# Layer 1's first feed-forward group: tiles 6 and 7 through seven block products instead of two plain projections

## The chip, the core and the metric

The kernel runs on one core of a Trainium2 chip, eight of which share the chip. A core has TensorE (matmuls into PSUM, eight banks of 512 fp32 columns), VectorE, ScalarE, GpSimd and SyncE, which work side by side, each through its own instructions in order, and DMA engines that move data between the chip's memory (HBM) and the on-chip SBUF. Nearly all transfers are issued from SyncE's queue (SP), which also runs in order. The metric is the device time of one execution in microseconds (us), the median over the runs.

## The reference

Two kinds of layers alternate, twice each, on x of 2048 tokens by 640 features in fp32: a linear attention with 32 heads of 20, and a feed-forward layer of width 1728 with squared ReLU. Both use the same weights each time.

```python
def attention(x, wqkv, wo):
    q, k, v = heads(x @ wqkv)                       # 32 heads of 20
    phi = lambda t: where(t > 0, t + 1, exp(t)) + 1e-6
    pq, pk = phi(q), phi(k)
    kv = einsum("bhsd,bhse->bhde", pk, v)
    z = einsum("bhsd->bhd", pk)
    den = einsum("bhqd,bhd->bhq", pq, z)[..., None] + 1e-6
    o = einsum("bhqd,bhde->bhqe", pq, kv) / den
    return merge(o) @ wo

def feed_forward(x, w1, b1, w2, b2):
    h = x @ w1 + b1
    return maximum(h, 0) ** 2 @ w2 + b2

for _ in range(2):
    x = x + attention(layernorm(x), wqkv, wo)
    x = x + feed_forward(layernorm(x), w1, b1, w2, b2)
```

## The kernel before

**Precision.** Matmuls take fp32 operands as pairs of a high part (rounded by a copy on ScalarE) and a low part (the difference, on VectorE); a product is three matmuls: high by high, high by low, low by high. "High half" and "low half" below mean these two copies.

**Tiles and groups.** A tile is 128 tokens; 16 tiles form 4 groups (g = 0 to 3) of 4. In a layer the attention first goes through all tiles for phi(k) and phi(q), storing phi(q) in HBM (`pqd`). A transition then makes kv and folds it with wo into one 640 x 640 matrix M, of which five row blocks `M[0..4]` are kept as high and low halves. The output projection of a tile is phi(q), divided by its denominator and transposed, times M. Group 0's four tiles are projected in the transition. The later groups are projected inside the feed-forward stage of the group before, between its chunks.

**A group's feed-forward.** The first stage runs 14 chunks (c = 0 to 13, `fc1` at L1336) of 128 hidden units, 15 matmuls of 512 columns each (10 in the last), each followed by two activations on ScalarE (`act`, L1357). The second stage runs 28 steps (`fc2_step`, L1581), seven products by four units, on sums of hidden blocks. Their weights come through a ring of six buffers of 640 KB (`load_ring`, L387), in the order that `uses_of` (L224) lists; a load is issued on SP as soon as a buffer's last matmul is done. In group 0 of each layer, seven further units are loaded once and stay (`load_stay`, L415).

**The order of the other work** is written by hand: `at(g, n, f)` (L1639) hangs a piece of work behind chunk n of group g (or behind step n - 14 of the second stage), and `("pe", n)` hangs matmuls directly behind chunk n, ahead of the rest. Pieces on one place run in the order of their registration, which is: the bias additions, the mixing of M (`mix_M`), the feed-forward's own splits, the single tiles, the pairs. "Step n" below is the place behind chunk n. `after(g)` (L1700) turns negative steps into steps of the stage before, except in group 0, where they become step 0.

**A tile of the next group** goes through: `b_load_pq` (phi(q) from HBM into one of eight buffers shared with other tiles of the same size, tag "f", L121), `b_den` (two instructions on VectorE), `b_blocks` (the division and a transpose of 32 x 32 blocks on VectorE), `blocks_move` (L520; 16 copies of 32 x 160 on ScalarE, in quarters of four), the split into halves, the projection, the addition to x, the layer norm, and a trip through HBM that spreads it for the next group's first stage.

- *Single* (`single`, L1660): tile i of a group is projected by 30 matmuls of 320 columns, behind chunk `b = OUTS[i]` = 4, 7, 10 or 13. Its phi(q) is loaded at b - 8, the denominator comes at b - 6, blocks and the first two quarters at b - 5, the others at b - 4, the halves at b - 3 and b - 2.
- *Pair* (`pair`, L1730, and `pairs`, L1845): tiles 2j and 2j + 1 of the group are taken as the upper and lower row of a 2 x 2 block matrix, two 128-column blocks wide to a block, M's first 512 rows as another 2 x 2; seven products of sums (a Strassen-Winograd form) replace eight, and the last 128 columns of phi(q) by `M[4]` ("rest") are added in plain form: 6 + 6 + 3, 6 + 9, 6 + 9, and 9 matmuls of 320 columns, behind chunks c0 + 4 to c0 + 7, where c0 = `PAIR_AT[j]` = 1 or 6. Sums of token blocks are made on VectorE and split in the steps from c0 + 1 on; sums of M's blocks come from HBM: units m6, m7 and m4 through the ring, and m5 in the place of M's right half columns (`place`).

**Mixing.** `mix_M(g)` (L1865) makes those sums of M once in a layer, on VectorE and GpSimd with scratch in hidden and x buffers, splits them and stores them to HBM, in steps 1 to 6 of group `MIX_G[layer]` when that is 0. `place` then loads m5 over M's right half.

**Which tiles are pairs** is set by `PAIR_FROM[layer]` = (group, j), L62: from there on, pairs. In layer 0 it is (1, 1), with the mixing in the same group 1: in that group two singles, then one pair. In layer 1 it was (1, 0), with the mixing in group 0: all four tiles of group 0's stage (tiles 4 to 7 of the layer) are singles, and `place` waits for the second stage.

Of the kernel before, what the change touches and what calls it, by code (L numbers as in the profile page):

```python
# [21 lines left out]
TG = 4  # L22
# [34 lines left out]
PQ_AT, DEN_AT, TURN_AT = (-7, -5, -3, -1), (-3.5, -1, 1, 3), (-2.5, 0, 2, 4)  # L57
# [1 line left out]
    ((-2, 0), (-1.5, 1), (-1, 2), (-0.5, 3)), ((0, 0), (1, 1), (1, 2), (2, 3)),  # L59
    ((3, 0), (4, 1), (5, 2), (5, 3)), ((6, 0), (6, 1), (7, 2), (7, 3)),  # L60
)
MIX_G, PAIR_FROM = (1, 0), ((1, 1), (1, 0))  # L62
BLOCKS = 5


def unit_range(k):
    return 2 * k, min(2 * k + 2, KH)
# [7 lines left out]
def kernel(  # L75
# [25 lines left out]
    def bank(i, n=1):  # L101
        return PS[:, 512 * i : 512 * (i + n)]
# [17 lines left out]
    def ftile(name):  # L120
        return tmp.tile([P, D], F32, tag="f", name=name, bufs=F_BUFS)  # L121
# [136 lines left out]
    for m in ORDER:  # L258
        for k in range(PAIRS):
            a, b = unit_range(k)  # L260
# [183 lines left out]
    def ln_stats(t, xt):  # L444
        st = small.tile([P, 2, 6], F32, tag="bn", name="bn")
        for j in range(2):
            nc.vector.bn_stats(st[:, j], xt[:, j * HD : (j + 1) * HD])
        mv = small.tile([P, 2], F32, tag="mv", name="mv")
        nc.vector.bn_aggr(mv, st)  # L449
        rs = small.tile([P, 1], F32, tag="rs", name="rs")  # L450
        (nc.vector if t == ("a", 0) and not xT else nc.gpsimd).tensor_scalar(  # L451
            rs, mv[:, 1:2], LN_EPS, None, op0=ALU.add
        )
        nc.gpsimd.tensor_tensor(out=rs, in0=rs, in1=neghalf, op=ALU.pow)
        sts[t] = mv, rs
# [64 lines left out]
    def blocks_move(yz, js):  # L520
        if len(yz) == 1:
            yz.append(ftile("z"))
        yv, zv = (a.rearrange("p (c j q) -> p c j q", c=DC, q=B32) for a in yz)
        for j in js:
            for i in range(P // B32):
                nc.scalar.activation(  # L526
                    zv[j * B32 : (j + 1) * B32, :, i, :], yv[i * B32 : (i + 1) * B32, :, j, :], AF.Copy
                )
# [29 lines left out]
    def mm3(ps, lh, ll, rh, rl, first, last):  # L558

        seq = [(lh, rh), (ll, rh), (lh, rl)]  # L560
        for i, (a, b) in enumerate(seq):
            nc.tensor.matmul(ps, a, b, start=first and i == 0, stop=last and i == 2)  # L562
# [58 lines left out]
    for layer in range(N_LAYERS):  # L621
# [157 lines left out]
        pq, xr, pT, yzp, yzx, xn = {}, {}, {}, {}, {}, {}  # L779
# [3 lines left out]
        def b_load_pq(t):  # L783
            if t < NT:
                pq[t] = ftile("pqt")
                nc.sync.dma_start(pq[t], pqd[t])
# [9 lines left out]
        def b_load_x(t):  # L796
            xr[t] = x1_at(t)
            nc.sync.dma_start(xr[t], src[t])
# [24 lines left out]
        def b_step(t, n=1):  # L823
            for _ in range(n):
                next(b_gen.setdefault(t, b_ops(t)), None)

        def b_den(t):
            b_step(t, 2)

        def b_blocks(t):  # L830
            b_step(t, 3)
# [121 lines left out]
        for t in range(NT):  # L953
# [54 lines left out]
            g = list(range(DC)) if t > 0 else []  # L1008
# [154 lines left out]
        def run_side(n=1):  # L1163
            for _ in range(min(n, len(side_work))):
                side_work.pop(0)()
# [129 lines left out]
        wu.free = 1 if layer == 0 else 3  # L1295
        wu.load_ring()
        b_load_pq(4)
        run_side(2)
        for i in (2, 3):
            po[i] = bank((2, 4)[i - 2], 2)  # L1300
# [29 lines left out]
        def f_bias(t):  # L1330
            nc.gpsimd.tensor_tensor(out=xr[t], in0=xr[t], in1=b2bc, op=ALU.add)
# [287 lines left out]
        def p_split(t, first=0):  # L1619

            u = pTs[:, t % 2]
            v = yzp[t][1]
            nc.scalar.activation(u[:, 0], v, AF.Copy)
            yield
            nc.vector.tensor_tensor(out=u[:, 1], in0=v, in1=u[:, 0].bitcast(F32), op=ALU.subtract)
            pT[t] = u
# [12 lines left out]
        def at(g, n, f):  # L1639
            events.setdefault((g, n), []).append(f)  # L1640
# [19 lines left out]
        def single(g, i):  # L1660

            t, b = TG * (g + 1) + i, OUTS[i]

            on = after(g)
            if t > TG:
                on(b - 8, lambda: b_load_pq(t))
            on(b - 6, lambda: b_den(t))
            on(b - 5, lambda: b_blocks(t))
            on(b - 5, lambda: blocks_move(yzp[t], (0, 1)))
            on(b - 4, lambda: blocks_move(yzp[t], (2, 3)))  # L1670
            sp = p_split(t)
            on(b - 3, lambda: next(sp, None))
            on(b - 2, lambda: next(sp, None))
            on(b - 3, lambda: b_load_x(t))
            ps = []

            def out():
                yzp.pop(t)
                for j in range(2):
                    s = slice(j * HD, (j + 1) * HD)  # L1680
                    ps.append(bank(6 + j)[:, :HD])
                    for c in range(DC):
                        a = pT[t][:, :, c * P : (c + 1) * P]
                        mm3(ps[j], a[:, 0], a[:, 1], M[c][:, 0, s], M[c][:, 1, s], c == 0, c == DC - 1)
                pT.pop(t)

            def add():
                for j in range(2):
                    v = xr[t][:, j * HD : (j + 1) * HD]
                    nc.vector.tensor_tensor(out=v, in0=ps[j], in1=v, op=ALU.add)  # L1690
                ln_stats(("b", t), xr[t])

            at(g, ("pe", b), out)
            on(b + 1 + 0.5 * (i == 3), add)
            on(b + 2, lambda: norm_out(t))
            on(b + 3, lambda: f_bias(t))

            x_in(g, i)

        def after(g):  # L1700
            def on(n, f):
                if n < 0 and g > 0:
                    at(g - 1, NF + N_STEPS + 2 * n, f)
                elif n >= NF:
                    at(g, NF + int(2 * (n - NF)), f)
                else:
                    at(g, max(n, 0), f)

            return on

        def norm_out(t):
            xn[t] = ftile("xn")
            ln_apply(("b", t), xn[t], xr[t])
            xd[t] = spread_out(xn.pop(t))

        def x_in(g, i):
            t = TG * (g + 1) + i

            def load():
                yzx[t] = spread_in(xd.pop(t))  # L1720

            n = NF + (1, 5, 9, 13)[i]
            at(g, NF + (0, 3, 7, 11)[i], load)
            steps(lambda: x_split(t), (g, n + 4), (g, n + 5), (g, n + 6))
# [120 lines left out]
        def pairs(g):  # L1845
            on = after(g)
            js = [j for j in range(2) if (g, j) >= PAIR_FROM[layer]]
            both = [pair(g, j) for j in js]
            for p in both:
                next(p)  # L1850
            for i, moves in enumerate(MOVES_AT):
                if i // 2 not in js:
                    continue
                t = TG * (g + 1) + i
                on(PQ_AT[i], lambda t=t: b_load_pq(t))
                on(DEN_AT[i], lambda t=t: b_den(t))
                on(TURN_AT[i], lambda t=t: b_blocks(t))
                for n, q in moves:
                    on(n, lambda t=t, q=q: blocks_move(yzp[t], (q,)))
                on(PAIR_AT[i // 2] + 1, lambda t=t: b_load_x(t))  # L1860
                x_in(g, i)
            for p in both:
                next(p, None)
# [136 lines left out]
        for g in range(NG - 1):  # L2000
            for i in [i for i in range(TG) if (g, i // 2) < PAIR_FROM[layer]]:
                single(g, i)
            if (g, 1) >= PAIR_FROM[layer]:
                pairs(g)
# [69 lines left out]
```

## Time and profile before

| | |
|---|---|
| median of 3 runs | 1308.28 us (1307.75 to 1308.47) |
| profiled execution's own time | 1307.57 us |
| its span | 1305.9 us |
| TensorE busy | 1300.7 us (100%) |
| VectorE / ScalarE / GpSimd busy | 964.2 / 748.0 / 239.1 us |
| layer 1, group 0, first stage | 898.79 to 962.94 us of the span |
| layer 1, group 0, second stage | 962.94 to 1005.18 us |

In the profile's lines PE is TensorE, PEld its weight loads, DVE VectorE, ACT ScalarE, POOL GpSimd and SPq the queue of SyncE. A line of the timeline has start and length in us, engine, line of the kernel, operation, output and input by the program's names, shapes, and in brackets how long the engine was idle before and what ended that. L526 is `blocks_move`, L517 the block transpose, L562 a single's matmuls, L1806 a pair's, L1351 a chunk's, L1595 the second stage's. The chain of work that ended last is followed back from the end of the execution through what released each piece.

### The profile page before, as it was taken

The page shows a single profiled execution, that of the slowest core. Times are in us where ns is not written, and L with a number is a line of the kernel's source. Part 1 is how long each engine was busy: PE and PEld are TensorE (multiplying, and loading weights), DVE is VectorE, ACT ScalarE, POOL GpSimd, SP SyncE. Part 2 cuts the span into 40 slices and gives each one's busy share as a digit, 9 for nine tenths or more (in the row PEclk, how much of TensorE's full clock was granted, in tenths as well). Part 3 has the DMA queues.
Part 4 walks back from the last instruction along what each step waited for, and adds up shares of the span by engine and source line. Part 5 has one row for each costly group of instructions (what it writes and reads, how often), then busy time and mean ns, then how long its engine had stood idle before and what let it go on. Part 6 is the DMA issues. An engine that isn't in the chain of part 4 may idle for free.

```text
span 1305.9 us, 21566 instructions
## 1 busy us (share of the span) xinstructions
PE 1300.7 (100%) x7534; PEld 1189.1 (91%) x7534; DVE 964.2 (74%) x1788; ACT 748.0 (57%) x1663; POOL 239.1 (18%) x304
## 2 busy tenths in 40 slices
PE   9999999999999999999999999999999999999998
PEld 8888899989988988998988889999899899889998
DVE  8888978767975976933867877587779479579565
ACT  5988958785385486334323332397755934944342
POOL 2333310064031102101012222102330030021000
PEclk9999999999999999999999999999999999999999
DMA  6898985699997986998968666544889779779976
GB/s 196 251 279 266 309 264 171 256 352 383 329 330 252 324 333 234 300 371 286 346 212 235 210 173 175 149 174 174 318 293 367 275 252 330 297 249 318 355 269 220
DMA packets 155426, 355.06 MB, mean 272 GB/s; under 512 B 18406, under 2 KB 77670, under 8 KB 154678
## 3 DMA queue, kind: packets, MB, share of 16 engines
q1 hardware_dynamic: 148086, 331.39, 74.7%
q0 software_dynamic: 7232, 22.29, 6.6%
q8 instruction: 60, 0.98, 0.3%
q14 instruction: 48, 0.39, 0.1%
HBM read 265.76 MB, written 76.02 MB: 262 GB/s over the span
## 4 chain that ended last, share of the span: by engine, by line
PE 100%; POOL 0%; DVE 0%; issue 0%; ACT 0%; POOLq 0%
PE PS L1351 26%; PE PS L1595 26%; PE PS L654 21%; PE PS L562 12%; PE PS L1806 4%; PE PS L589 3%; PE PS L1467 3%; PE PS L703 2%; PE PS L1197 1%; PE PS L1185 1%; PE PS L976 1%; PE PS L715 0%; PE PS L463 0%; PE PS L1138 0%; PE PS L478 0%; DVE x L1609 0%
## 5 line engine op out<-in xcount | busy, mean ns | idle before, releaser
L1351 PE MATMUL PS<-xTb,u 128*128 128x512 f32 x1490 | 345.8, 390 | 0.0
L1351 PEld LDWEIGHTS PS<-xTb,u 128*128 128x128 f32 x1490 | 277.8, 188 | 56.1 <-issue 0.3
L654 PE MATMUL PS<-kq,xT 128*128 128x320 f32 (+2 forms) x1575 | 283.9, 334 | 0.0
L654 PEld LDWEIGHTS PS<-kq,xT 128*128 128x128 f32 x1575 | 250.3, 188 | 27.5 <-DVE rl L675 1.0
L1595 PE MATMUL PS<-u,arena 128*128 128x320 f32 x1644 | 250.6, 309 | 0.0
L1595 PEld LDWEIGHTS PS<-u,arena 128*128 128x128 f32 x1644 | 243.4, 188 | 0.4
L526 ACT ACTIVATE z<-y 32x160 f32<-32x160 f32 x512 | 171.1, 334 | 41.5 <-DVE y L517 35.5
L1567 ACT ACTIVATE arena<-R 128x512 fp32r<-128x512 f32 (+1 forms) x200 | 115.4, 591 | 122.4 <-PE PS L1595 84.7
L1576 DVE TENSOR_TENSOR arena<-R,arena 128x512 fp32r<-128x512 f32 (+1 forms) x200 | 136.2, 688 | 45.3 <-ACT arena L1567 43.3
L562 PE MATMUL PS<-kh,xh 128*128 128x512 f32 x480 | 124.3, 393 | 0.0
L451 POOL TENSOR_SCALAR rs<-mv 128x1 f32<-128x1 f32 x63 | 31.0, 492 | 469.5 <-DVE mv L449 468.8
L1362 ACT ACTIVATE R<-PS,b1sb 128x512 f32<-128x512 f32 x94 | 64.6, 687 | 88.0 <-PE PS L1351 87.2
L1595 PE MATMUL PS<-uw,arena 128*128 128x320 f32 x660 | 106.1, 309 | 0.0
L562 PEld LDWEIGHTS PS<-kh,xh 128*128 128x128 f32 x480 | 87.3, 188 | 15.3 <-DVE xT L578 0.2
L1595 PEld LDWEIGHTS PS<-uw,arena 128*128 128x128 f32 x660 | 99.1, 188 | 0.3 <-DVE x L1609 0.2
L1541 DVE TENSOR_TENSOR R<-R 128x512 f32<-128x512 f32 (+1 forms) x128 | 88.5, 693 | 8.5 <-ACT R L1363 8.5
L550 ACT ACTIVATE z<-y 32x160 f32<-32x160 f32 x260 | 86.9, 334 | 4.9 <-DVE y L532 1.9
L667 ACT ACTIVATE r<-PS 128x512 f32<-128x512 f32 (+1 forms) x64 | 27.7, 434 | 88.2 <-PE PS L654 81.8
L1609 DVE TENSOR_TENSOR x<-PS,x 128x320 f32<-128x320 f32 x112 | 52.9, 483 | 18.8 <-PE PS L1595 18.1
L1817 DVE TENSOR_TENSOR x<-PS,x 128x320 f32<-128x320 f32 x56 | 27.1, 489 | 52.6 <-PE PS L1806 51.8
L1363 ACT ACTIVATE R<-R 128x512 f32<-128x512 f32 x94 | 59.5, 633 | 3.0
L674 DVE TENSOR_SCALAR r<-r 128x512 f32<-128x512 f32 (+1 forms) x64 | 21.2, 332 | 51.9 <-ACT r L667 51.9
(191 smaller groups left out, 1684.4 us busy)
## 6 DMA issues: line engine op xcount, KB each, us to landing
u<-kept SPq DMA_DIRECT2D x113, 640.0 KB
u<-kept_w SPq DMA_DIRECT2D x97, 640.0 KB
u<-kept SPq DMA_DIRECT2D x56, 320.0 KB
kept<-uprep SPq DMA_DIRECT2D x49, 320.0 KB
u<-kept_m SPq DMA_DIRECT2D x21, 640.0 KB
z<-xb SPq DMA_DIRECT2D x160, 80.0 KB
pqt<-pq SPq DMA_DIRECT2D x32, 320.0 KB
acc<-r POOLq DMA_DIRECT2D x28, 320.0 KB, 5.4
```

Source lines behind the costliest of these rows:

```text
L526: nc.scalar.activation(zv[j * B32 : (j + 1) * B32, :, i, :], yv[i * B32 : (i + 1) * B32, :, j, :], AF.Copy)
L550: nc.scalar.activation(dst, blk, AF.Copy)
L562: nc.tensor.matmul(ps, a, b, start=first and i == 0, stop=last and i == 2)
L654: nc.tensor.matmul(ps, xT[t][:, k, c, :], kq[c][:, l, a:b], start=(k, c, l) == seq[0], stop=(k, c, l) == seq[-1],)
L1351: nc.tensor.matmul(ps, a[:, d, :], bb[:, d, :], start=(d, i) == order[0], stop=(d, i) == order[-1],)
L1362: nc.scalar.activation(r, v, AF.Relu, bias=b1sb[:, c : c + 1])
L1363: nc.scalar.activation(r, r, AF.Square)
L1541: nc.vector.tensor_tensor(out=quad(*out, k), in0=quad(*x, k), in1=quad(*y, k), op=op)
L1567: nc.scalar.activation(u[:, 0], v, AF.Copy)
L1576: nc.vector.tensor_tensor(out=u[:, 1], in0=v, in1=u[:, 0].bitcast(F32), op=ALU.subtract)
L1595: nc.tensor.matmul(ps, x, y, start=opens and k == 0 and p == 0 and e == 0, stop=k == PAIRS - 1 and p == b - a - 1 and e == len(seq) - 1, s ...
L1609: nc.vector.tensor_tensor(out=v, in0=ps, in1=v, op=ALU.add)
```

## The change

`PAIR_FROM[1]` becomes (0, 1): in layer 1's group 0, tiles 4 and 5 stay singles and tiles 6 and 7 become a pair. From that follows:

- the ring gets three more units in that stage, m6, (chunk 13's weights,) m7, m4, by `uses_of`; the second stage's first six ring units stand behind them;
- `place` moves to step 7 of group 0, behind tile 5's projection;
- tile 6's and 7's work moves from a single's steps to a pair's: phi(q) loaded at step 0 (was 2 and 5), denominators at steps 2 and 3 (was 4 and 7; `max(DEN_AT[i], 2)` keeps tile 6's from step 1), blocks at 2 and 4 (was 5 and 8), moves in quarters at 3 to 5 and 6 to 7 (was 5 to 6 and 8 to 9), x loaded at 7 (was 7 and 10), products behind chunks 10 to 13;
- `soon` is true in layer 1 alone. Tile 5's phi(q) is then loaded in the transition, right behind tile 4's. In group 0 the singles' denominators, blocks and moves come a step sooner (`a = b - 1`): tile 5's at 0, 1, 1 and 2 instead of 1, 2, 2 and 3. Tile 4's were at step 0 and stay there. The splits and projections keep their steps.

Nothing changes in layer 0.

```diff
-MIX_G, PAIR_FROM = (1, 0), ((1, 1), (1, 0))
+MIX_G, PAIR_FROM = (1, 0), ((1, 1), (0, 1))
...
         b_load_pq(4)
+        soon = PAIR_FROM[layer] == (0, 1)
+        if soon:
+            b_load_pq(5)
         run_side(2)
...
-            if t > TG:
+            if t > TG + soon:
                 on(b - 8, lambda: b_load_pq(t))
-            on(b - 6, lambda: b_den(t))
-            on(b - 5, lambda: b_blocks(t))
-            on(b - 5, lambda: blocks_move(yzp[t], (0, 1)))
-            on(b - 4, lambda: blocks_move(yzp[t], (2, 3)))
+            a = b - (soon and g == 0)
+            on(a - 6, lambda: b_den(t))
+            on(a - 5, lambda: b_blocks(t))
+            on(a - 5, lambda: blocks_move(yzp[t], (0, 1)))
+            on(a - 4, lambda: blocks_move(yzp[t], (2, 3)))
...
-                on(DEN_AT[i], lambda t=t: b_den(t))
+                on(max(DEN_AT[i], 2) if g == 0 else DEN_AT[i], lambda t=t: b_den(t))
```

## The prediction

> **What bounds the kernel now.** I read the page's busy times first, then the chain of work that ended last, then that chain in order of time, then the two feed-forward stages of layer 1's group 0 and of layer 0's group 1 as windows.
>
> ```profile
> span 1305.9 us, 21566 instructions
> PE 1300.7 (100%) x7534; PEld 1189.1 (91%) x7534; DVE 964.2 (74%) x1788; ACT 748.0 (57%) x1663; POOL 239.1 (18%) x304
> PEclk9999999999999999999999999999999999999999
> PE 100%; POOL 0%; DVE 0%; issue 0%; ACT 0%; POOLq 0%
> ```
>
> TensorE works without a gap from start to end at full granted clock. So the time is the sum of the matmuls, and an edit counts only if it removes matmuls or makes TensorE wait. The chain in order of time, for layer 1's group 0 (before the change four tiles by 30 matmuls each; two of them shown) and for layer 0's group 1 (two tiles so, then a pair by products in four groups; two shown):
>
> ```profile
> 930.44 4.39 PE PS L562 x30
> 934.83 10.22 PE PS L1351 x45
> 945.06 4.39 PE PS L562 x30
> ...
> 404.70 2.19 PE PS L1806 x15
> 410.32 2.19 PE PS L1806 x15
> ```
>
> Columns: start, length, what. 30 matmuls of 320 columns take 4.39 and 15 take 2.19, 146 ns each. The windows hold TensorE's, the weight loads', VectorE's, ScalarE's and GpSimd's busy time, the clock, the DMA share and GB/s:
>
> ```profile
> 358.44:421.75 63.31, 63.31 (x321) 55.17 (x321) 39.31 (x76) 48.21 (x113) 17.54 (x19) 1.00 0.82 290
> 421.75:464.08 42.33, 42.33 (x289) 42.25 (x289) 41.17 (x72) 16.98 (x33) 5.96 (x7) 1.00 1.03 334
> 898.79:962.94 64.15, 64.15 (x328) 56.06 (x327) 45.89 (x72) 47.00 (x107) 26.95 (x26) 1.00 0.85 306
> 962.94:1005.18 42.24, 42.24 (x289) 42.24 (x289) 40.19 (x71) 18.96 (x37) 3.83 (x6) 1.00 0.94 312
> 940.00:950.00 10.00, 10.00 (x57) 9.01 (x56) 7.00 (x14) 6.72 (x15) 3.24 (x4) 1.00 1.04 417
> ```
>
> Layer 0's group 1 already has the form that layer 1's group 0 gets: the stage is 0.84 shorter, the next one 0.09 longer. It is the pattern, except that it could begin its tiles' work in the stage before.
>
> **The change part by part.** *Matmuls.* Tiles 6 and 7 lose 2 x 30 and get 15 + 15 + 15 + 9 = 54, so 6 x 0.146 = 0.88 go. From layer 0's second stage I take 0.1 back: 0.78 net, if nothing is late.
>
> *What TensorE waits for then.* The first products (1, 5, the rest product) stand behind chunk 10, at 934.83 + 10.22 = 945.05; before, tile 6's 30 matmuls stood there and needed tile 6 alone. Now the second half of tile 7 must have been moved, and two sums split, by then. The path is ScalarE: its queue holds the 32x160 moves, 16 to a tile, between the chunk activations.
>
> ```profile
> 904.71 5.53 ACT L526 ACTIVATE z<-y 32x160 f32<-32x160 f32 x16 [1.10 <-DVE y L517]
> 910.27 0.69 ACT L1362 ACTIVATE R<-PS,b1sb 128x512 f32<-128x512 f32 x1
> 911.53 0.73 ACT L1623 ACTIVATE pTs<-z 128x640 fp32r<-128x640 f32 x1
> 912.16 0.67 ACT L1362 ACTIVATE R<-PS,b1sb 128x512 f32<-128x512 f32 x1
> 916.39 2.77 ACT L526 ACTIVATE z<-y 32x160 f32<-32x160 f32 x8 [2.89 <-DVE y L517]
> 920.44 1.45 ACT L1899 ACTIVATE arena<-R 128x640 fp32r<-128x640 f32 x3
> 927.81 0.72 ACT L1899 ACTIVATE arena<-x 128x640 fp32r<-128x640 f32 x1
> 929.34 0.47 ACT L1899 ACTIVATE arena<-x 128x320 fp32r<-128x320 f32 x1 [0.31 <-DMA kept_m<-arena]
> 935.21 0.62 ACT L1567 ACTIVATE arena<-R 128x512 fp32r<-128x512 f32 x1
> 396.75 2.75 ACT L526 ACTIVATE z<-y 32x160 f32<-32x160 f32 x8
> 399.53 0.69 ACT L1362 ACTIVATE R<-PS,b1sb 128x512 f32<-128x512 f32 x1
> ```
>
> Starts to next starts give: 16 moves 5.56, 8 moves 2.78 (396.75 to 399.53), 4 moves 1.39; a chunk's two activations 1.26 (910.27 to 911.53); a tile's high half 0.63; the first three splits of mixed weights 1.46, the second three 2.00 (927.81 to 929.81, with 0.31 of waiting for a store); a unit's high half 0.64; that of a sum 0.43, between a move and a unit. The new queue in order from 904.71: tile 4's moves 5.56; chunk 1 1.26; tile 4's high half 0.63; two quarters of tile 5 2.78; chunk 2 1.26; two more 2.78; chunk 3 1.26; mixed splits 1.46; tile 6's first quarter 1.39; chunk 4 1.26; tile 5's high half 0.63; second quarter 1.39; chunk 5 1.26; mixed splits 2.00; the last two quarters 2.78; chunk 6 1.26; unit 0.64; two quarters of tile 7 2.78; chunk 7 1.26; unit 0.64; high half of sum 1 0.43; two quarters 2.78. Sum 37.5: tile 7 is ready at 942.2. In layer 0 its last moves ended at 399.50, which is 939.85 when shifted by the two stages' starts (540.35).
>
> From there ScalarE does chunk 8 (1.26) and a unit's high half (0.64), and VectorE takes that unit's low half and gets to the low half of sum 5:
>
> ```profile
> 401.44 0.69 DVE L1576 TENSOR_TENSOR arena<-R,arena 128x512 fp32r<-128x512 f32 x1 [1.48 <-DMA x<-in_A_x_dram]
> 403.17 0.42 DVE L1756 TENSOR_TENSOR pTs<-z,pTs 128x256 fp32r<-128x256 f32 x1
> 403.85 0.48 DVE L1770 TENSOR_TENSOR pTs<-z,pTs 128x128 fp32r<-128x128 f32 x2
> 408.10 0.76 DVE L1756 TENSOR_TENSOR pTs<-z,pTs 128x256 fp32r<-128x256 f32 x2
> ```
>
> 401.44 to 403.59 is 2.15, so sum 5's low half ends 942.2 + 1.26 + 0.64 + 2.15 = 946.25. Product 5's second matmul asks for it at 945.05 + 7 x 0.146 = 946.07: **a wait of about 0.2**. The rest product's low halves end 2.89 behind 401.44 in layer 0, so here at 947.0; it asks for the second of them some 0.88 behind 946.25, at 947.1: even. With waking up I put 0.3. Bounds: 0, if ScalarE comes as early as in layer 0 (2.3 sooner), and 2.2, if its 37.5 of queue run 5% longer. I take 0.3, since every term but the order is a row of this stage. The later products have room: in layer 0 even the third group's low halves (408.10 to 408.86) were there 1.46 before the second group began (410.32).
>
> *What must be on time ahead of it.* Tile 5's phi(q): before, VectorE waited for it, and ScalarE for VectorE (the 2.89 above). It is now loaded in the transition, behind tile 4's (879.84), into a buffer whose last reader, the first turn of x, ends at 880.5; SP then has nothing to issue until 892.03, so the load costs nothing there. (Tile 5's buffer shifts the later ones by one; the last late tile's comes to follow a store issued at 892.03 and is written at 895.97. Transfers have stopped by 894: share 0.00.) That lets the denominator of tile 5 follow tile 4's turn:
>
> ```profile
> 879.69 0.84 DVE L517 STREAM_TRANSPOSE y<-xn 128x640 f32<-128x640 f32 x1
> 879.84 0.32 SPq L786 DMA_DIRECT2D pqt<-pq  x1
> 904.60 1.52 DVE L1879 TENSOR_TENSOR R<-uM 128x640 f32<-128x640 f32 x2
> 908.09 1.23 DVE L803 TENSOR_TENSOR y<-pqt,zbc 128x640 f32<-128x640 f32 x1 [1.97 <-DMA pqt<-pq]
> 913.03 0.86 DVE L812 TENSOR_SCALAR den<-den 128x32 f32<-128x32 f32 x1
> 915.51 0.84 DVE L517 STREAM_TRANSPOSE y<-pqt 128x640 f32<-128x640 f32 x1
> 892.03 9.06 SPq L1125 DMA_DIRECT2D pq<-rl  x3
> 895.97 0.44 ACT L667 ACTIVATE rl<-PS 128x320 f32<-128x320 f32 x1 [0.94 <-PE PS L654]
> 894.00:895.00 1.00, 1.00 (x9) 1.00 (x8) 0.10 (x1) 1.00 (x2) 0.78 (x2) 1.00 0.00 0
> ```
>
> 904.60 + 2.07 (denominator: 1.23 as in its row and a reduction of as many elements, put at 0.84) + 1.52 (mixing sums) + 3.32 (the rest and the turn beside GpSimd, 913.03 to 916.35) = 911.5, ahead of ScalarE's 912.2. If the load were late by more than 0.7, ScalarE would be late by the excess. Tile 6's and 7's loads go to step 0 on SP, behind the bias and ahead of the next chunk's weights; tile 5's, issued there, landed by 908.09, and VectorE asks for tile 6's at about 913.5. The mixing on GpSimd starts 2 later, hidden up to ScalarE's first split of it at 920.3, where it stood before too. Tile 6 is turned at 911.5 + 1.5 (second mixing sums) + 0.8 (tile 4's low half) + 2.07 + 3.32 = 919.2, and ScalarE gets to it at 921.7; tile 7, behind the mixed low halves (at most 2 after 921.7), by 927, against 934.4. The reordered tail gives VectorE 7 low halves, 2 short ones, 4 sums and 3 more additions, 16 instructions of 0.5 at most, for two low halves of a tile, in a stage where it is idle for 64.15 - 45.89 = 18.3, and takes tile 7's addition out of the next.
>
> *DMA.* Three units of 640 KB (m6, m7, m4), and the two halves of M that `place` overwrites, 2 x 320 KB, move ahead of the products.
>
> ```profile
> 928.88 1.03 SPq L413 DMA_DIRECT2D u<-kept_w  x1
> 934.10 0.61 SPq L1909 DMA_DIRECT2D kept_m<-arena  x1
> ```
>
> m6 cannot be read before the second mixed store, issued to 934.7; it and the M halves follow. Queued from 928.9: 640 + 1280 (store) + 640 (a resident unit) + 640 + 640 KB = 3.93 MB, at 306 GB/s (the stage's mean) to 417 (its best row) 9.4 to 12.8: M's halves land by 942, needed at 945.9. m7 and m4 are issued behind chunks 9 and 10 (941.7, 945.1) and needed at 956 and 961. The second stage's first unit is issued behind chunk 11 (950.7), no longer behind chunk 8, and needed at 963.8. Hidden, with 4 or more to spare; if that cover went, each us late would be one us of TensorE.
>
> The Trainium skill (ScalarE: Activation LUTs, What ACT_TABLE_LOAD costs) gives an ACTIVATE with immediates 186 ns + 0.833 ns per element, overlapping the one before by about 93 ns: 226 ns per move, an estimate. This trace has 16 in 5.53, 346 ns each, so the overlap isn't seen here. By the page the 64 moves would be 7.7 shorter, nothing would wait, and the time would be that of no wait below.
>
> **Sum.** -0.88 + 0.1 + 0.3 = **-0.5**: the profiled execution (1307.57) would take 1307.1. The median of the runs, 1308.28, is 0.7 above it: **1307.8**.
>
> **The rivals.** *No wait at all* (ScalarE is as early as in layer 0): -0.78, 1307.5. For: the same pattern there shows none. Against: 2.3 of later start.
> *Tile 7 late, slower than before*: the last quarter of tile 7 ends after 942.0, and TensorE waits us for us at product 5. From 942.8 the gain is gone. The queue has no idle place left; if the second mixed splits wait 3 longer for the first store's DMAs (0.31 now) the sum is 945.2, the wait 3.3, the time 1308.28 - 0.78 + 3.3 = 1310.8; with 2 more of contention, 1312.8. For: a DMA share of 1.04 from 940 on. Against: that store's stretch is less loaded than before, tile 7's phi(q) load having moved out of it.
> *M's halves or m6 late*: they queue behind a store and a resident unit. 7 later than 942 would be a wait of 3, 1310.5. Against: the sizes above.
> *The change doesn't do what it says*: tile 4's step sooner falls away, being clamped to step 0; if tile 5's load also stayed late, ScalarE would lose the 2.89 again: wait 3.1, 1310.6.
>
> The Trainium skill (TensorE: Matmul & The Clock Gate, What's actually happening) holds that an idle window of about 3.4 us halves the clock; it would put some 2 us more on the worst of these. No row here shows such an idle, and the wait I forecast is far shorter.
>
> **How the numbers follow.** Forecast (wait under 1) 0.58; no wait 0.20; tile 7 late 0.12; M or m6 late 0.06; load still late 0.04. Two runs of this kernel tell apart about 0.2%, 2.6: 1305.7 to 1310.9. Even with no wait the gain is under 0.9, so faster by more has 0.02, for something unseen. The slower cases (0.22) are priced close to 1310.9 with contention still to add, so two thirds of them are put beyond it: 0.15. Same 0.83. The range: 1306.8 (no wait, on the profiled execution's own time) to 1310.2 (a wait of 2.7: the 5% bound and a little of the first late case).
>
> **What would show it.** Right: 54 matmuls in place of 60 in a stage of 63.3 to 63.8; tile 7's last moves ending near 942.2 of this time scale; a gap below 1 behind product 1 and nowhere else; second stage 42.3. Wrong: ScalarE idle between 905 and 942, a gap that ends on a DMA into M or u, a second stage longer than 42.5, or any difference before 898.79.

## The result, and the profile after

The changed kernel takes 1310.34 us (median of 15 runs, 1309.13 to 1312.96); the kernel before, beside it on the same chip, 1308.28 (15 runs, 1307.12 to 1309.84). The ratio is 1.0018, 95% interval 1.0011 to 1.0026: 2.1 us slower, where 0.5 less was forecast, and 0.14 above the top of the range. The profiled execution took 1311.45.

The page's span and busy times, and the shares in the chain that ended last:

```profile
span 1309.6 us, 21593 instructions
PE 1301.7 (99%) x7528; PEld 1189.2 (91%) x7528; DVE 969.4 (74%) x1803; ACT 749.1 (57%) x1670; POOL 240.4 (18%) x304
PE 92%; DVE 3%; ACT 2%; DMA 2%; issue 1%; POOL 0%; SPq 0%; ACTq 0%; POOLq 0%; DVEq 0%
```

The six matmuls are gone (7528 for 7534), yet TensorE's busy time is 1.0 longer, and the chain, which was all TensorE, now runs 8% of the span elsewhere (the work that it follows back from the waits, not idle time of TensorE). So TensorE waited, and some of its matmuls became slower. The windows say in which stage (columns as in the prediction: length; TensorE, weight loads, VectorE, ScalarE, GpSimd; granted clock, DMA share, GB/s):

```profile
898.65:966.75 68.10, 65.09 (x322) 56.32 (x321) 49.69 (x84) 48.62 (x114) 26.25 (x24) 0.97 0.83 300
966.75:1009.10 42.35, 42.35 (x290) 42.22 (x289) 41.16 (x72) 16.94 (x33) 5.95 (x7) 1.00 1.02 335
948.00:950.00 2.00, 1.19 (x4) 0.81 (x4) 1.00 (x3) 1.19 (x3) 2.00 (x1) 0.62 1.01 307
950.00:952.00 2.00, 2.00 (x8) 1.96 (x9) 0.95 (x2) 0.42 (x1) 1.94 (x3) 0.53 1.04 407
948.00:948.50 0.50, 0.13 (x1) 0.16 (x2) 0.50 (x2) 0.47 (x2) 0.50 (x1) 0.97 1.13 338
948.50:949.00 0.50, 0.50 (x3) 0.50 (x3) 0.50 (x2) 0.50 (x2) 0.50 (x1) 0.50 0.91 305
```

All of it is in the first stage of layer 1's group 0: 68.10 against 64.15, with TensorE idle for 3.01 of it. The second stage is 0.11 longer. The timeline of TensorE names the place:

```profile
944.76 1.04 PE L1810 MATMUL PS<-uM,pTs 128*128 128x320 f32 x6
948.37 1.04 PE L1810 MATMUL PS<-uM,pTs 128*128 128x320 f32 x3 [2.57 <-ACT R L1365]
949.86 1.97 PE L1810 MATMUL PS<-uM,pTs 128*128 128x320 f32 x6 [0.45 <-DMA uM<-kept_m]
951.62 3.71 PE L1354 MATMUL PS<-xTb,u 128*128 128x512 f32 x15
955.17 1.04 PE L1810 MATMUL PS<-u,pTs 128*128 128x320 f32 x6
957.37 3.59 PE L1354 MATMUL PS<-xTb,u 128*128 128x512 f32 x15
```

Product 1 runs; then product 5, whose weights are the two halves of M that `place` overwrites, waits twice. Its first three matmuls need the first half, the next three the second. Start to start, the group of 15 products takes 6.86 (944.76 to 951.62) in place of 15 x 0.146 = 2.19, so 4.67 too long: 3.02 of waiting, and 1.65 mostly because the matmuls behind the first wait are slow: the clock falls to 0.62 and 0.53 for two windows, and six matmuls take 1.97 where six take 1.04 at 955.17. In windows of 0.5 (the last two rows above) it is 0.97 from 948.0 and 0.50 from 948.5, so it falls ahead of the second wait; it is at 1.00 again from 952.0. The next chunk loses 0.13 more (3.55 from start to start, 3.42 for the one behind it). 4.67 + 0.13 - 0.88 = 3.9, which is what the stage is longer.

The ScalarE walk and the arithmetic behind it came out within 0.4 of the forecast (ScalarE, then VectorE):

```profile
904.57 5.54 ACT L526 ACTIVATE z<-y 32x160 f32<-32x160 f32 x16 [1.09 <-DVE y L517]
912.01 2.75 ACT L526 ACTIVATE z<-y 32x160 f32<-32x160 f32 x8
928.12 0.74 ACT L1903 ACTIVATE arena<-x 128x640 fp32r<-128x640 f32 x1 [0.42 <-DMA kept_m<-arena]
939.75 2.75 ACT L526 ACTIVATE z<-y 32x160 f32<-32x160 f32 x8
```

```profile
944.43 0.69 DVE L1579 TENSOR_TENSOR arena<-R,arena 128x512 fp32r<-128x512 f32 x1 [1.48 <-ACT arena L1570]
945.64 0.61 DVE L459 TENSOR_SCALAR xn<-x,mv,rs 128x640 f32<-128x640 f32 x1
946.17 0.42 DVE L1760 TENSOR_TENSOR pTs<-z,pTs 128x256 fp32r<-128x256 f32 x1
```

Tile 5's moves begin at 912.01 without a wait (forecast 912.2), tile 7's last end at 942.50 (942.2), and the low half of sum 5 ends at 946.59 (946.25). TensorE goes on only at 948.37. The releaser that the row names for the 2.57, a chunk activation, is not what product 5 reads: its token operand had been there for 1.8. What was missing is seen in the queue of SP and in the chain:

```profile
926.80 0.75 SPq L422 DMA_DIRECT2D uw<-kept  x1
929.75 2.50 SPq L1911 DMA_DIRECT2D kept_m<-arena  x2
933.19 0.79 SPq L1913 DMA_DIRECT2D kept_m<-arena  x1
934.03 1.48 SPq L422 DMA_DIRECT2D uw<-kept  x1
942.26 0.33 SPq L413 DMA_DIRECT2D u<-kept_m  x1
942.67 1.47 SPq L1916 DMA_DIRECT2D uM<-kept_m  x2
```

```profile
SPq L413 <- DMA kept_m<-arena: 6.7, 1, 6.7
SPq L422 <- DMA uM<-kept_m: 0.6, 1, 0.6
```

```profile
932.34 9.84 DMA kept_m<-arena
942.26 0.33 SPq L413
...
943.57 6.25 DMA uM<-kept_m
```

The second view is what SP waited for (total, times, longest), the third the chain in order of time. The last piece of the second mixed store is issued by 933.98, and one resident unit behind it. Then SP stands for 6.7: the next in its queue is the load of m6, which reads what that store writes, and it is issued only when the store has landed, at 942.26.

By the chain it is the piece issued at 932.34 that it waits for: 9.84 from issue to landing. M's halves come behind m6. The first has landed by 948.2, where an issue of SP that waited for it goes out (the view's second row, at 948.25), and product 5 begins at 948.37; the second lands at 949.8, 7.8 later than the 942 of the prediction. The gap ends on a DMA into M, which the prediction had named as a sign of being wrong. Why the store itself took so long is what the first experiment asks.

### The profile page after: what moved, and what is told of

Read it like the earlier page. It is cut to its first block, busy times and chain, and to the rows that moved or that the text cites. A ratio compares the mean times of both kernels' runs of the same rounds, so it can differ in the third digit from the quotient of the medians.

```text
span 1309.6 us, 21593 instructions
## 1 busy us (share of the span) xinstructions
PE 1301.7 (99%) x7528; PEld 1189.2 (91%) x7528; DVE 969.4 (74%) x1803; ACT 749.1 (57%) x1670; POOL 240.4 (18%) x304
## 4 chain that ended last, share of the span: by engine, by line
PE 92%; DVE 3%; ACT 2%; DMA 2%; issue 1%; POOL 0%; SPq 0%; ACTq 0%; POOLq 0%; DVEq 0%
PE PS L1598 26%; PE PS L1354 23%; PE PS L654 19%; PE PS L562 10%; PE PS L1810 5%; PE PS L1470 2%; PE PS L703 2%; PE PS L589 1%; ACT z L526 1%; DMA kept_m<-arena 1%; PE PS L1185 1%; PE PS L976 1%; PE PS L1197 1%; DMA uM<-kept_m 0%; ACT z L550 0%
## 5 line engine op out<-in xcount | busy, mean ns | idle before, releaser
L1821 DVE TENSOR_TENSOR x<-PS,x 128x320 f32<-128x320 f32 x64 | 31.0, 488 | 62.0 <-PE PS L1810 59.1
L1612 DVE TENSOR_TENSOR x<-PS,x 128x320 f32<-128x320 f32 x112 | 52.9, 483 | 18.8 <-PE PS L1598 18.1
```

## The experiments

The theory: M's halves are late, because SP holds them back behind m6, which waits for a store that a backlog of transfers delays. The rivals: product 5 waits for ScalarE and VectorE after all (the releaser named in the row); tile 6's later denominator, or tile 5's load and earlier turn, cost something by themselves.

### The resident units four chunks later (stays_late, stays_late_2)

The changed kernel, with the seven resident units of layer 1 begun behind chunk 7 instead of chunk 3, so that fewer transfers stand ahead of the store:

```diff
-                if g == 0 and 3 <= c:
+                if g == 0 and (7 if last_layer else 3) <= c:
                     wu.load_stay()
```

> The changed kernel, with layer 1's seven resident units loaded from step 7 of group 0 on instead of step 3, so behind the second mixed store, m6 and M's halves. Theory M (TensorE's wait of 3.0 in the changed kernel is M's right half arriving at 948 to 950, because SP stood until 942.3 for the second mixed store, whose packets were behind the resident units' loads; the lower granted clock afterwards follows from the idle): the store is done by about 937, M's halves land by 943, TensorE waits at most 0.4 at product 5, for the low half of the sum, the clock stays at 1.00, the time is 1307.4 to 1308.2. Theory S (the wait is for ScalarE and VectorE, as the release of most of it by an activation says; the DMA decided the last 0.45 only): 2.6 of wait stay, 1309.5 to 1310.5. A third way: the resident units now come too late for the second stage, and TensorE waits there instead, 1310 or more.

The first profiled execution took 1308.32. Its SP queue and TensorE:

```profile
933.67 1.06 SPq L1913 DMA_DIRECT2D kept_m<-arena  x1
937.03 0.33 SPq L413 DMA_DIRECT2D u<-kept_m  x1
```

```profile
947.34 1.43 PE L1810 MATMUL PS<-uM,pTs 128*128 128x320 f32 x8 [0.93 <-DVE pTs L1760]
```

The store is issued no earlier (to 934.73), but m6 goes out 2.3 behind that instead of 8.3, so 5.2 earlier. The wait for M is gone; 0.93 for the low half of sum 5 is left, and the clock stays at 1.00. With fewer bytes queued around the store the stall is gone, and ScalarE's and VectorE's work is as it was. The median is no better, though: 1310.13 (11 runs, 1308.32 to 1315.02), ratio 1.0013 (1.0003 to 1.0022). So it ran again:

> stays_late once more, for its profile: its first profile had a wait of 0.93 in all and 1308.32, while its median was 1310.13. If the late resident units (their loads start a step later in layer 1's group 0, and reach into the second stage) are what makes the median slow, a profile near 1310 shows TensorE waiting for a DMA of a unit in the second stage or the next chunks, 1 to 2 in all. If the DMA of M's halves is still late by chance in most runs, it shows the wait at product 5 behind product 1 again, 2 or more, and the fallen clock. If the profile is again near 1308.3 and clean, it stays open.

Median 1310.08 (12 runs), ratio 1.0013 (1.0005 to 1.0022), and this time the profiled execution (1310.18) is a typical one. The wait at product 5 is again 0.83, from VectorE. A window inside the second stage, and what SP waited for in that stage:

```profile
976.00:994.00 18.00, 17.36 (x112) 16.19 (x111) 17.36 (x33) 8.91 (x16) 0.03 (x1) 1.00 1.01 288
```

```profile
SPq L413 <- DMA u<-kept: 11.9, 9, 1.8
```

TensorE runs 112 matmuls there where the kernel before runs 124, and the stage takes 44.04 instead of 42.24. SP stands 11.9 there for units on their way, against 6.5 in the kernel before and 7.1 in the first profile, whose second stage took 42.37. The last resident unit is now issued at 963.75 (948.25 in the changed kernel), among the ring's units for this stage. So the loss has moved some 30 us on, which fits the third way that was expected; that the delayed units cause it is not shown. One row of TensorE names a late unit (0.22 at 993.23), and soon_only, which delays no unit, has such a wait too (0.46 at 992.02).

### M's halves ahead of m6 (place_first, place_first_2)

The changed kernel, with one thing altered: behind chunk 7 of that stage the ring's next load (m6) is issued after the step's other work, so that `place` comes first on SP.

```diff
-                wu.load_ring()
+                hold = last_layer and (g, c) == (0, 7)
+                if not hold:
+                    wu.load_ring()
                 act(c, ps)
                 run(g, ("pe", c))
                 run(g, c)
+                if hold:
+                    wu.load_ring()
```

> The changed kernel, with the loads of M's right halves issued ahead of m6's at step 7. Theory M: SP stands only for the part of the second mixed store that holds m5, issued first, so M's halves are issued 1 to 2 sooner, TensorE waits 1 to 2, too short for the clock to fall, 1308.5 to 1309.5. Theory S: no change against the changed kernel, 1310.3.

1308.19 (11 runs, 1307.29 to 1308.95), ratio 0.9995 (0.9987 to 1.0004); again on another chip 1308.51, ratio 1.0001 (0.9992 to 1.0009).

```profile
934.25 6.17 SPq L1916 DMA_DIRECT2D uM<-kept_m  x2
942.18 0.32 SPq L413 DMA_DIRECT2D u<-kept_m  x1
```

```profile
947.29 1.44 PE L1810 MATMUL PS<-uM,pTs 128*128 128x320 f32 x8 [0.72 <-DVE pTs L1760]
```

The first half is issued at 934.25, since it comes from the first store; the second waits 3.3 for its part of the second store and is out by 940.42, 3.7 before the changed kernel's (944.14). m6 goes out when it did, and its own product comes so much later that nothing waits for it. TensorE waits 0.72, for the low half of sum 5, less than the 1 to 2 that was expected, and the clock does not fall. This is the whole loss: 2.1 to 2.7 us go with the order of three loads in one queue. ScalarE and VectorE were not touched, so the rival that names them for the long wait falls.

> place_first once more, so that the two kernels above are compared with it on one chip: a wait of 0.5 to 1 behind product 1, 1307.9 to 1308.6.

In that run ScalarE's second mixed splits wait for the first store, 0.53 here and 0.33 at the third of them, where the prediction had 0.31 in all:

```profile
928.73 0.74 ACT L1903 ACTIVATE arena<-x 128x640 fp32r<-128x640 f32 x1 [0.53 <-DMA kept_m<-arena]
```

### Tile 5's soon-load and earlier turn, alone and taken away (soon_only, stays_late_no_soon)

First that part of the change alone, on the kernel before:

```diff
+        soon = last_layer
+        if soon:
+            b_load_pq(5)
...
-            if t > TG:
+            if t > TG + soon:
                 on(b - 8, lambda: b_load_pq(t))
+            a = b - (soon and g == 0 and i < 2)
-            on(b - 6, lambda: b_den(t))
+            on(a - 6, lambda: b_den(t))
...
```

> The kernel before (four single tiles in group 0), with tile 5's phi(q) loaded in the transition and its denominator, blocks and moves a step sooner, nothing else. The prediction put this part at nothing: 1307.9 to 1308.7, no gap on TensorE. If the early load or the shifted buffers cost something in the transition, 1309 or more, with a gap between 880 and 905.

1308.53 (11 runs), ratio 0.9994 (0.9985 to 1.0003): nothing, neither gained nor lost. Its trace has no gap between 880 and 905.

Then stays_late without it:

```diff
-        soon = PAIR_FROM[layer] == (0, 1)
+        soon = False
```

> As stays_late, but tile 5's phi(q) is loaded at step 0 and its steps are those of before. The walk through ScalarE's queue says that ScalarE stands about 2.9 for tile 5, tile 7's last moves end at 945, and TensorE waits about 3 for sum 5 at product 5, with the clock possibly falling after it: 1310 to 1312. If the queue has room that the walk did not see, or M decides alone: as stays_late, 1307.4 to 1308.2.

1314.75 (5 runs, 1312.92 to 1316.78), ratio 1.0045 (1.0032 to 1.0058), which is 4.6 above stays_late and more than was expected.

```profile
948.54 0.41 PE L1810 MATMUL PS<-uM,pTs 128*128 128x320 f32 x1 [1.44 <-ACT pTs L1756]
950.42 2.22 PE L1810 MATMUL PS<-uM,pTs 128*128 128x320 f32 x8 [1.47 <-DVE pTs L1760]
```

```profile
918.19 2.77 ACT L526 ACTIVATE z<-y 32x160 f32<-32x160 f32 x8 [3.80 <-DVE y L517]
952.00:954.00 2.00, 2.00 (x7) 1.71 (x6) 1.90 (x6) 1.29 (x4) 2.00 (x1) 0.50 1.03 386
```

ScalarE loses 3.80 at tile 5 (2.89 in the kernel before), and everything behind it in its queue is late. Not all of it arrives: the mixed splits, now later, stand 0.96 less, and counted from the stage's start tile 7's last moves end 2.5 behind those of stays_late (946.28 - 899.51 and 943.19 - 898.96). Product 5 waits 2.91 for the second sum's halves, where it waited 0.93. The clock falls to 0.50 behind it, which adds to it. So the soon-load is worth nothing by itself and 4.6 in the place where ScalarE's queue sets the end.

### Tile 6's denominator a step sooner (den_early)

place_first with `max(DEN_AT[i], 2)` undone, so that tile 6's denominator is at step 1 again:

```diff
-                on(max(DEN_AT[i], 2) if g == 0 else DEN_AT[i], lambda t=t: b_den(t))
+                on(DEN_AT[i], lambda t=t: b_den(t))
```

> As place_first, with tile 6's denominator at step 1 again, the step of layer 0. The prediction's walk has ScalarE as the later one at tile 5's and 6's moves: no change against place_first, 1307.8 to 1308.6. If the denominator, now ahead of tile 5's turn on VectorE or of the mixing, holds ScalarE up, tile 7's last moves end 0.5 to 2 later and TensorE waits as much longer.

1308.14 (11 runs), ratio 0.9995 (0.9986 to 1.0004), against 1308.51 for place_first_2 beside it: no difference that two medians can tell. Its trace has no wait at the products, but its stage also begins 0.7 later (899.69 for 898.98), a lag that TensorE has in the transition already (869.87 for 869.15), while ScalarE's second mixed splits, held by the first store in one (0.86 in all) and hardly in the other (0.27), begin within 0.1 of each other (928.80, 928.73). TensorE comes later and ScalarE doesn't, so the absent wait cannot be put down to the denominator.

### The pair's work ahead of the feed-forward's on each step (pair_ahead)

place_first, with layer 1's singles and pair of group 0 registered ahead of the feed-forward's own splits, so that the low half of sum 5 does not stand behind a unit's:

```diff
+        if soon:
+            single(0, 0)
+            single(0, 1)
+            pairs(0)
         for g in range(NG):
             ffn_events(g)
-        for g in range(NG - 1):
+        for g in range(1 if soon else 0, NG - 1):
```

> As place_first, and layer 1's single tiles and pair of group 0 are registered ahead of the feed-forward's own splits, so that on each step ScalarE and VectorE do the pair's splits first: the low half of sum 5 no longer stands behind a unit's low half, a sum of hidden blocks and a layer norm (2.15 in the walk). What is left of TensorE's wait in place_first (0.72) is that order: it goes, unless M's second half lands later than 946.7; 0 to 0.3 of wait, 1307.3 to 1308.0, 0.5 to 0.7 under place_first. If the feed-forward's own units come too late for it, the wait is found behind chunk 13 or in the second stage, and nothing is gained.

A miss: 1311.38 (11 runs), ratio 1.0024 (1.0015 to 1.0032). The low half of sum 5 is in time, but now an addition of sums lies beside GpSimd's bias additions:

```profile
944.86 0.42 DVE L1760 TENSOR_TENSOR pTs<-z,pTs 128x256 fp32r<-128x256 f32 x1 [0.34 <-ACT pTs L1756]
945.20 3.71 DVE L1753 TENSOR_TENSOR z<-z 128x256 f32<-128x256 f32 x1
```

```profile
945.54 3.07 POOL L1334 TENSOR_TENSOR x<-x,b2bc 128x640 f32<-128x640 f32 x2
949.37 0.56 PE L1810 MATMUL PS<-uM,pTs 128*128 128x320 f32 x2 [2.09 <-DVE pTs L1774]
```

The same addition takes 0.42 at 942.53 in the changed kernel, where GpSimd does no addition of this kind. In the last row TensorE waits 2.09 for the rest product's low half, which is queued behind that addition on VectorE. No run takes GpSimd's additions away alone, so that they are the cause is not shown. This edit moves other work of the stage too (its second stage takes 43.29), so its time is not the price of one operation.

### Tile 5's layer norm a step later (place_first_norm)

place_first, with the 0.61 that stands ahead of sum 5's low half on VectorE (945.64 above) moved to the next step:

```diff
-            on(b + 2, lambda: norm_out(t))
+            on(b + 2 + (soon and g == 0 and i == 1), lambda: norm_out(t))
```

> The kernel with M's halves issued ahead of the unit (place_first), and tile 5's layer norm of layer 1's group 0 (and with it its store to be spread) a step later, step 10 in place of step 9. Theory: what is left of the wait at product 5, 0.7 to 0.8, is VectorE's queue: the low half of sum 5 stands behind the layer norm's 0.61 (946.26 in place_first's profile). With that gone the wait is 0.1 to 0.3 and the time 0.5 lower: 1307.7 to 1308.1, at or a little below the kernel before. Rival: ScalarE's last moves set the sum themselves, so that VectorE would wait in the layer norm's place: wait unchanged, 1308.2 to 1308.5. Second rival: the store of tile 5, a step later, comes late for the second stage's first turn of x, a wait there of up to 1: 1308.5 to 1309.2.

1308.30 (11 runs), ratio 0.9998 (0.9989 to 1.0007).

```profile
945.37 2.70 PE L1810 MATMUL PS<-uM,pTs 128*128 128x320 f32 x15
947.92 3.59 PE L1354 MATMUL PS<-xTb,u 128*128 128x512 f32 x15
962.76 1.92 PE L1598 MATMUL PS<-uw,arena 128*128 128x320 f32 x12
```

No wait is shown any more. From the first chunk's start (899.11) to the second stage's 962.76 it is 63.65, 0.50 less than before and 0.64 less than place_first (64.29). Still missing to 0.88 is 0.38, and 0.36 of that is in the same group: 2.55 from start to start for its 15 matmuls. In the median the gain does not show.

### The changed kernel once more (after_again)

> The changed kernel once more, beside the next ones on one chip. Theory M: the load of m6 again stands for the second mixed store until about 942, M's halves land at 948 to 950, TensorE waits 2 to 3.5; runs in which the clock falls after it are 1 to 2 longer than runs in which it doesn't; 1309.5 to 1311 in the median. If the first profile was an exception, no wait over 1 and 1308.

1311.17 (11 runs, 1309.28 to 1313.40), ratio 1.0021 (1.0012 to 1.0030): the same result on another chip. This profiled execution took 1309.52, and its waits were shorter:

```profile
946.87 0.80 PE L1810 MATMUL PS<-uM,pTs 128*128 128x320 f32 x3 [0.81 <-ACT R L1366]
948.40 1.14 PE L1810 MATMUL PS<-uM,pTs 128*128 128x320 f32 x6 [0.74 <-DMA uM<-kept_m]
```

The place is the same and the clock stays at 1.00. m6 was issued at 941.75, 0.5 sooner than in the first profile. The runs of both series split by the granted clock over the whole execution: 12 of 26 at 1.000, with medians 1309.94 and 1309.5, and 14 at 0.997 to 0.999, with medians 1311.58 and 1311.74. So the clock seems to fall in about half of the runs. That is a sign and no count, since the kernel before, without such a wait, has 0.999 in 3 of 33 runs beside these.

The 1.6 to 2.2 between the halves need not be the clock alone. In the two profiles the group of 15 products takes 6.86 and 4.36 (945.02 to 949.38), of which 3.02 and 1.55 are waiting. What is left above 2.19 is 1.65 and 0.62, so the fallen clock costs about 1.0 there, with the next chunk's 0.13 about 1.2, and the longer waiting 1.5.

## Why the prediction was wrong

**Matmuls: right.** Six fewer, and the second stage 0.11 longer by the windows (0.1 forecast).

**ScalarE's walk: right.** 37.9 from start to end (904.57 to 942.50) for 37.5. Its error of 0.4 is the wait for the first mixed store, 0.7 to 0.9 in all (0.42 and 0.31, 0.53 and 0.33) for 0.31. The kernel without soon-load shows the other side of it: a late turn goes through to TensorE, less what the queue regains. What the prediction says of the overlap holds for the moves alone: its row at 911.53 runs 0.73, to 912.26, and the next instruction starts at 912.16.

**The wait at sum 5: right place, size too small.** 946.25 - 946.07 was 0.18, and 0.3 was taken; 0.72 to 0.93 is left where M is in time. VectorE's 2.15 holds (944.43 to 946.59 is 2.16). ScalarE's walk is 0.4 longer, and the start of the products was read from the chain, 945.06, which counts a matmul from the end of the one before it; the timeline of the kernel before has it at 944.90:

```profile
944.90 1.33 PE L562 MATMUL PS<-uM,pTs 128*128 128x320 f32 x8
```

0.18 + 0.4 + 0.16 = 0.74. A part of the 2.15, tile 5's layer norm, could have been seen to be movable: a step later, the wait is no longer shown.

**The soon-load costs nothing: right**, alone 0.9994 (0.9985 to 1.0003), and the wait without it was near the forecast (3.1, measured 2.91), in part by luck: the kernel without the soon-load lost more at tile 5 than the 2.89 of the forecast, 3.80, and arrived with 2.5 of it, on a wait that was already 0.93 and not 0.2.

**DMA: the step that failed.** It read: "Queued from 928.9: 640 + 1280 (store) + 640 (a resident unit) + 640 + 640 KB = 3.93 MB, at 306 GB/s (the stage's mean) to 417 (its best row) 9.4 to 12.8: M's halves land by 942, needed at 945.9", and "Hidden, with 4 or more to spare". They landed at 949.8. It has two errors. The sum starts in mid-queue: of what was issued from 925.5 to 929.0 it counts one unit, and leaves out a tile of x and three units, 320 + 3 x 640 KB = 2.3 MB. At the 337 GB/s of the window 925.5 to 928.9 no more than 1.1 MB can have moved by then; the other 1.2 MB are some 3 to 4 us at the prediction's rates, an estimate.

The second error is that it treats the chain as one stream of bytes, though it said itself that m6 cannot be read before the store. A load of what a store writes is not queued behind it: SP waits until the store has landed, then issues, and then the bytes have to move. So there are two passes through full queues, one behind the other: 9.84 from issue to landing of the store's piece for m6 (932.34 to 942.18), then 7.1 for M's halves behind m6 (942.67 to 949.8). Fewer bytes around the store (stays_late) or another order of issue (place_first), each alone, take the wait for M away. Layer 0 had shown the wait in the kernel before:

```profile
389.55 1.22 SPq L1909 DMA_DIRECT2D kept_m<-arena  x1
394.11 0.33 SPq L413 DMA_DIRECT2D u<-kept_m  x1
```

```profile
SPq L413 <- DMA kept_m<-arena: 3.3, 1, 3.3
```

There, the halves were issued 10 before their product (394.53 and 404.54), so 3.3 cost nothing. In layer 1 the same code has fewer us between store and product, and the resident units of group 0, which layer 0's group 1 doesn't have, ahead of the store. The Trainium skill (DMA: Bandwidth & Descriptors, Two DMAs through the same engine are not ordered) says that the issuing engine has to wait for the first transfer's completion before it issues one that depends on it, sharing a queue being no substitute. The trace agrees: 6.7 and 3.3 of waiting on SP.

The rival "M's halves or m6 late" was this mechanism, with 1310.5 against 1310.34 measured, at a chance of 0.06: set aside by "the sizes above", while it is an order of issue that decides. That its price meets the median is luck. It had one wait of 3 in every run and a full clock; the two profiles have 1.55 and 3.02 of waiting, a slow restart behind it, and in one of them a clock that falls.

**The clock: set aside too early.** The prediction took the rule of the Trainium skill (TensorE: Matmul & The Clock Gate, What's actually happening), an idle window of about 3.4 us before the clock is halved, as out of reach. Here 2.57 in one piece was enough: the clock is at 0.50 from 948.5, ahead of the 0.45. In stays_late_no_soon 1.44 and 1.47 with one matmul between were; 2.09 alone (pair_ahead) and 0.81 with 0.74 were not. So the halving agrees with the Trainium skill, and the idle time that brings it can be shorter than its window and, in one trace, broken by a matmul. The prediction's "some 2 us more on the worst of these" is above the 1.2 that the two profiles give.

**What stays open.** Whether the pair pays at all: with both waits gone the stage is 0.50 shorter in place_first_norm's profile, and 0.35 with the second stage (den_early's stage, where no wait shows either, is 0.63 shorter), but no version was faster than the kernel before by more than the intervals hold (place_first 0.9987 to 1.0004, place_first_norm 0.9989 to 1.0007). Why those 15 matmuls still take 0.36 more wasn't tried.

## What to carry to other kernels

Where a load reads what an earlier DMA writes, price it as two passes: from the store's issue to its landing behind all that is queued since the last time the queues were empty, and then the load's own way; and price everything behind it on the issuing queue with it, since that queue stands meanwhile. Put the loads that depend on nothing, on an older store, or on a piece that is issued sooner, ahead of the one that waits: here this order alone was worth 2.1 to 2.7 us. When a transfer is to be made earlier by delaying others, look where the others then land: with the resident units delayed, the next stage lost 1.8 in the second profile and the median gained nothing.

## What the runs showed of the hardware

- The load of m6 went out 9.9 after the issue of the 320 KB piece of the store that it waits for (932.34 to 942.26, the changed kernel), and 4.1 after it (932.98 to 937.03, stays_late) with two 640 KB units fewer issued just ahead of the store and one fewer behind.
- The granted clock fell to 0.50 for about 3.4 us, by windows of 0.5: at 948.5, right behind an idle time of 2.57 in one piece (the changed kernel), and at 950.8, 0.4 behind the second of two of 1.44 and 1.47 with one matmul between (stays_late_no_soon). It stayed at 1.00 after 2.09 in one piece and after 0.81 + 0.74.
- An addition of 128 x 256 on VectorE took 3.71 beside two additions on GpSimd (3.07), and 0.42 without.
